# A segment-recurrent attention kernel: the last transpose and sum of each segment in two column halves, and the order of every engine written down whole

## The chip, the cores and the metric

The kernel runs on one core of one Trainium2 chip. The metric is device time in microseconds (us), from one launch to its end. Each kernel is run several times, and the median is compared.

## The reference

The input is 2048 tokens of 512 values. They go through a layer norm, then through an attention that runs over 64 segments of 32 tokens, one after the other, and at the end through a layer norm and an MLP. What matters here is the loop over the segments:

```python
mem = mem0                                            # 8 memory rows of 512
for s in range(64):
    h = concatenate([mem, x[32*s:32*s+32]])           # 40 rows
    q, k, v = h @ Wq, h @ Wk, h @ Wv                  # 32 heads of 128
    p = softmax(where(mask, q @ k.T * scale, -1e9))   # per head
    o = (p @ v) @ Wo                                  # 40 rows of 512
    mem = o[:8]                                       # feeds the next segment
    outs.append(o[8:])
```

The mask lets every row see the memory rows and, among the other 32, those up to itself. A segment can't begin before the memory rows of the one before are there; its other rows need nothing of it. Behind the loop stand `h = x + attention` and `h + MLP(layernorm(h))` with 1792 hidden values.

## The kernel before, in words

A segment has 8 memory rows (M) and 32 rows of x. 24 of the 32 (A) share a 32-row tile `hT` with the memory rows: `hT[:, slot, chunk, 0:24]` are x, `24:32` memory, with the 512 features in four chunks on the partitions. The last 8 x rows of four segments (B) are put together into one 32-row tile `hB`. So work goes by blocks of four segments, and the number of a segment modulo four is called its class here.

On TensorE (PE in the profile) a segment is a sequence of units. A unit of a projection is four matmuls of 512 columns, one per quarter of the array, over one of the four feature chunks. Each of Q0, Q1, K0, K1, V0, V1 (half of the heads each) is four such units on `hT`. F0 and F1 are units on `hB` or `OTB` that belong to the next block: its K in class 0, its Q in class 1, its V in class 2, and in class 3 the output projection of the B rows. They depend on nothing in the segment and fill gaps. SC0 and SC1 are the scores of the memory rows, PV0 and PV1 the products of their softmax with V, WO is the output projection (8 units of 16 matmuls of 256 columns), SA the scores of the A rows, and PVA their product with V, which belongs to the segment before: the A and B rows run one or more segments late, since only the memory rows are awaited.

The other engines carry results between these units. VectorE (DVE) and ScalarE (ACT) cast PSUM into SBUF (`kq`, `VS`, `OT`); VectorE transposes (`KALL`, `QT`, `PTC`, `PTA`, `QTB`). Names with m, x and B stand for the memory, A and B rows of one tile. The softmax of a half r (0 or 1) of the heads is, in order: `nmc` (negative maximum, VectorE), two Exps into `EC` (ScalarE; the code calls the parts Ea and EC), `rsc` and `PC` twice each (reciprocal, product), and `PTC` (transpose). The mask is copied into the scores' bank ahead of them (called SP0, SP1, for SA SAp). At the end of a segment VectorE transposes the result of WO out of PSUM into `TT` and adds the two halves of the heads with `halves_add`; the sums of the memory rows (called hTm) are written into the next segment's `hT`, those of the A rows (opA) into `opT`, later. GpSimd (POOL) does small copies (`ZC`, `BD`), the product `PA`, and the sums of `TTB`, the same result for the B rows, into `opT`. From there a DMA transpose (`oN`) takes a block back to rows of x.

All of this is recorded first, and a scheduler written in Python sets each engine's order before any instruction is emitted. TensorE's order is a table, `ORDERS`, one row a class, of (name, first unit, last unit). `PLAN` gives for many kinds of operation a due time in us after the segment's Q0, for each class; a segment counts `STEP` = 10.28. `HOME` pins a kind to an engine where two could do it, and the rest is decided by free time in the scheduler's own model. Some operations are kept back and recorded again behind another one (lists `late`, `now`, `turned`, `folds`). Each operation waits on a semaphore for what it reads; on its own engine too, for VectorE and GpSimd.

`align` counts TensorE's instructions and adds weight loads (the LDWEIGHTS without a matmul) until the first unit of a segment stands at a fixed place, modulo 256 instructions: `PHASE` = 0, 64, 128, 192 for classes 0 to 3. `KEEP` leaves out the weight load where the unit before has loaded the same chunk (`matmul_kept`, L606 in the profile).

Lines in the profile of before: L873 and L606 projections; L891 to L893 casts; L914 transposes of Q and K; L1042 scores; L1050 to L1069 softmax; L1080 and L1085 PV; L1110 to L1137 SA, its softmax, and `PTA`, `BD`; L1148 PVA; L1176 WO; L1188 the transpose into `TT`; L1182 every `halves_add`; L1219 to L1232 the B rows' sums; L1246 to L1260 the way back to rows.

Of the kernel before, what the change touches and what calls it, by code (L numbers as in the profile page):

```python
# [1694 lines left out]
```

## Time and profile before

| | |
|---|---|
| runs | 805.17, 806.22, 806.32 us; median 806.22 |
| profiled execution, first to last instruction | 804.0 us, 2.2 below the median |
| busy | PE 96%, DVE 77%, ACT 68%, POOL 44% of the span |
| until segment 1 begins | 51.96 us |
| segments 1 to 62 | 637.53 us (51.96 to 689.49), 10.28 each |
| last segment, MLP, output | 114.5 us |
| granted TensorE clock | 0.996 of full speed |

The profile shows one execution. In a row of the time line stand the start and the length in us, the engine, the line of the kernel, the operation, and what is written from what. Matmuls overlap in the records, so the distance between two starts tells more than a length. In a row of a group, the last numbers are the busy time in us with the mean of one in ns, and the idle time ahead of them.

### The profile page before, as it was taken

How to read it: one execution, taken by the hardware profiler on the slowest of the kernel's cores; microseconds unless marked ns; L12 is line 12 of the kernel's file. 1: busy time of each engine (PE TensorE's matmuls, PEld its weight loads, DVE VectorE, ACT ScalarE, POOL GpSimd, SP SyncE). 2: the span in 40 equal slices, each digit the busy share in tenths (PEclk: the TensorE clock that was granted, in tenths of full speed). 3: DMA queues.
4: the chain of work that ended last, by engine and by line, in shares of the span. 5: the costliest groups of instructions: out<-in, count | busy, mean ns of one | idle time of the engine just before them, and what ended most of it. 6: DMA issues, size and time to landing. Idle time of an engine off the chain costs nothing.

```text
span 804.0 us, 43669 instructions
## 1 busy us (share of the span) xinstructions
PE 772.7 (96%) x19317; PEld 419.3 (52%) x18821; DVE 616.6 (77%) x1975; ACT 543.0 (68%) x1618; POOL 350.7 (44%) x886
## 2 busy tenths in 40 slices
PE   3788999999999999999999999999999999999998
PEld 1345555555555555555555555555555555544443
DVE  3267898898989898998989898989898887824211
ACT  2456777777777777777777787777777777743342
POOL 5023334545454545454545454545463535367200
PEclk9999999999999999999999999999999999999999
DMA  9960010110101010101010102020212131264200
GB/s 338 393 188 16 4 30 11 27 34 23 37 18 42 18 43 14 46 10 47 8 50 10 49 11 51 10 51 3 51 29 63 37 87 32 89 167 132 69 27 26
DMA packets 65450, 48.04 MB, mean 60 GB/s; under 512 B 29028, under 2 KB 61676, under 8 KB 65260
## 3 DMA queue, kind: packets, MB, share of 16 engines
q1 hardware_dynamic: 64928, 44.98, 18.9%
q8 instruction: 150, 2.46, 1.3%
q14 instruction: 40, 0.33, 0.1%
q10 hardware_dynamic: 332, 0.27, 0.1%
HBM read 31.08 MB, written 8.13 MB: 49 GB/s over the span
## 4 chain that ended last, share of the span: by engine, by line
PE 91%; DVE 3%; DMA 2%; SPq 2%; ACT 1%; issue 0%
PE ps L873 43%; PE ps L1176 16%; PE ps L606 7%; PE quad L1584 6%; PE ps L1577 5%; PE ps L1215 4%; PE quad L1080 3%; DMA WQ<-in_A_Wq_dram 2%; SPq L776 2%; PE ps L1110 2%; PE quad L1042 2%; PE ps L1370 2%; PE quad L1148 1%; PE quad L1085 1%; DVE PC L1067 1%; ACT kq L891 1%
## 5 line engine op out<-in xcount | busy, mean ns | idle before, releaser
L873 PE MATMUL ps<-WQ,hT 128*32 128x512 bf16 x2048 | 157.0, 382 | 3.5 <-DVE hT L1182 3.3
L1176 PE MATMUL ps<-WO,OT 128*32 128x256 bf16 x4224 | 141.5, 275 | 1.0 <-ACT OT L891 1.0
L873 PE MATMUL ps<-WV,hT 128*32 128x512 bf16 x1780 | 138.1, 379 | 0.0
L892 ACT ACTIVATE kq<-ps 128x512 bf16<-128x512 f32 x146 | 87.2, 597 | 57.5 <-PE ps L873 57.2
L1131 POOL TENSOR_TENSOR PA<-SA,rsa 128x256 bf16<-128x256 f32 x64 | 39.8, 622 | 181.4 <-DVE rsa L1124 169.6
L891 ACT CAST kq<-ps 128x512 bf16<-128x512 f32 x160 | 93.3, 583 | 29.8 <-PE ps L873 29.8
L1176 PEld LDWEIGHTS ps<-WO,OT 128*32 128x32 bf16 x4224 | 96.2, 96 | 23.6 <-ACT OT L891 4.0
L1137 POOL COPY BD<-PTA 32x192 bf16<-32x192 bf16 x256 | 95.7, 374 | 16.5 <-DVE PTA L1133 0.8
L1067 DVE SCALAR_TENSOR_TENSOR PC<-EC,rsc,even 128x128 bf16<-128x128 f32 x256 | 94.5, 370 | 6.7
L873 PE MATMUL ps<-WK,hT 128*32 128x512 bf16 x1292 | 92.3, 379 | 0.0
L873 PEld LDWEIGHTS ps<-WQ,hT 128*32 128x32 bf16 x2048 | 56.4, 96 | 63.7 <-issue 19.3
L914 DVE STREAM_TRANSPOSE KALL<-kq 128x256 f32<-128x256 f32 x160 | 70.5, 441 | 21.3 <-ACT kq L891 19.0
L891 ACT CAST VS<-ps 128x512 bf16<-128x512 f32 x189 | 83.9, 444 | 0.9
L1059 ACT ACTIVATE EC<-quad,nmc 128x64 f32<-128x64 f32 x252 | 76.8, 310 | 5.7
L606 PE MATMUL ps<-WK,hT 128*32 128x512 bf16 x756 | 74.3, 379 | 0.0
L891 ACT CAST OT<-quad 128x128 bf16<-128x128 f32 (+1 forms) x208 | 68.4, 352 | 4.9 <-PE quad L1085 0.7
L914 DVE STREAM_TRANSPOSE QT<-kq 128x256 f32<-128x256 f32 x128 | 57.0, 446 | 16.1 <-ACT kq L892 15.0
L873 PEld LDWEIGHTS ps<-WV,hT 128*32 128x32 bf16 x1780 | 49.4, 96 | 34.9 <-issue 1.0
L1580 ACT ACTIVATE WQ<-ps,b1t 128x512 bf16<-128x512 f32 x42 | 28.9, 687 | 52.0 <-PE ps L1577 52.0
L1122 ACT ACTIVATE SA<-SA 128x256 f32<-128x256 f32 x64 | 26.7, 417 | 52.2 <-DVE SA L1121 48.8
L873 PEld LDWEIGHTS ps<-WK,hT 128*32 128x32 bf16 x1292 | 35.9, 97 | 46.6 <-issue 20.2
L1228 POOL TENSOR_TENSOR opT<-TTB,TTS 32x64 bf16<-32x64 f32 x128 | 40.3, 315 | 31.7 <-DVE opT L1182 22.5
(159 smaller groups left out, 1475.9 us busy)
## 6 DMA issues: line engine op xcount, KB each, us to landing
WV<-in_A_Wv_dram SPq DMA_DIRECT2D x4, 1024.0 KB, 10.4
WK<-in_A_Wk_dram SPq DMA_DIRECT2D x4, 1024.0 KB, 18.1
WQ<-in_A_Wq_dram SPq DMA_DIRECT2D x4, 1024.0 KB, 19.4
WO<-in_A_Wo_dram SPq DMA_DIRECT2D x16, 256.0 KB, 7.7
v_last<-VSB SPq DMA_DIRECT2D x60, 64.0 KB, 3.1
VBD<-v_last SPq DMA_DIRECT2D x60, 64.0 KB, 2.9
h_mid<-xr SPq DMA_DIRECT2D x16, 128.0 KB, 1.8
WQ<-h_mid SPq DMA_DIRECT2D x4, 512.0 KB, 4.4
```

What stands on the lines that cost most here:

```text
L606: return e.add_instruction(mybir.InstMatmult(name="I-%d" % (4000000 + _kept[0]), engine=mybir.EngineType.PE, start_tensor_calc=start, stop ...
L873: ins = e.matmul(o, l, m, start=(k == 0), stop=(k == DC - 1), tile_position=(0, 32 * j), skip_group_check=True)
L891: return {"act": (lambda e: e.copy(out, src), t_act(n, ps_)), "dve": (lambda e: e.tensor_copy(out, src), 0.155 + 1.0e-3 * n * fast)}
L892: return {"act": (lambda e: e.mul(out, src, scale_), t_act(n, ps_)), "dve": (lambda e: e.tensor_scalar(out, src, scale_, None, ALU.mult), ...
L914: S.op("dve", lambda e: e.transpose(out, src), reads=[("kq", i)], writes=[key], dur=t_dve(256) + 0.02)
L1059: return e.activation(EC[:, r, sl, :], o[:, sl, :], ACTF.Exp, bias=nmc[:, r, sl:sl + 1], accum_out=smc[:, r, sl:sl + 1])
L1067: S.op("dve", lambda e, sl=sl, xc=xc: e.scalar_tensor_tensor(PC[:, r, :, :, sl], xc, rsc[:, r, sl:sl + 1], ev, ALU.mult, ALU.mult), reads= ...
L1137: S.narrow(S.op("pool", lambda e, j=j, rows=rows: e.tensor_copy(BD[rows, par, :, j, :, :], PTA[rows, :, 0:NA, :]), reads=["PTA"], writes=[ ...
L1176: ins = e.matmul(ps[bank][32 * j:32 * j + 32, 0:256], lhs(slot(h)), wo_cols(h, b), start=(k == 0), stop=(k == 15), tile_position=(0, 32 * ...
L1228: return e.tensor_tensor(o[32 * q:32 * q + 32, c:c + 2], x, y, ALU.add)
L1577: ins = e.matmul(ps[bank][:, 0:SBT], W1[:, cc, fc * P:(fc + 1) * P], hnT_of(k)[:, cc, :], start=(cc == 0), stop=(cc == DC - 1))
L1584: S.op("pe", lambda e: e.matmul(quad[:, t, :], gT_of(k, fc)[:, t * P:(t + 1) * P], W2[:, fc, :], start=(fc == 0), stop=(fc == FC - 1)), re ...
```

## The change

1. The last step of a segment in halves. `wo` transposes columns 0 to 127 of the result, sums the memory rows of feature chunks 0 and 1 from them, and does the same for columns 128 to 255 and chunks 2 and 3. The keys of both are split, and the units of Q0, Q1 and K0 ask only for the half that their chunk lies in (`early`). `ORDERS` puts the units of chunks 0 and 1 of Q0 and K0 first.

```diff
-            S.op("dve", lambda e: e.transpose(tt..., ps[bank][:, 0:256]), reads=[("ps", bank)], writes=[("TT", par)], ...)
-            if mem:
-                sl = (s + 1) % RING
-                S.op("dve", lambda e: [halves_add(tt, q2, hT[64 * q2:64 * q2 + 64, sl, :, NA:SEG], slice(NA, SEG))(e) for q2 in range(2)][1],
-                     reads=[("TT", par)], writes=[("hTm", sl)], dur=0.4)
+            sl = (s + 1) % RING
+            for n in range(2):
+                c = slice(2 * n, 2 * n + 2)
+                S.op("dve", lambda e, n=n, c=c: e.transpose(tt[:, c]..., ps[bank][:, 128 * n:128 * n + 128]), reads=[("ps", bank)],
+                     writes=[("TT", par, n)], ...)
+                if mem:
+                    S.op("dve", lambda e, c=c: [halves_add(tt[:, c], q2, hT[64 * q2:64 * q2 + 64, sl, c, NA:SEG], slice(NA, SEG))(e) for q2 in range(2)][1],
+                         reads=[("TT", par, n)], writes=[("hTm", sl, n)], dur=0.36)
...
-                u = S.op("pe", f, reads=[(key, r, cc) for _, key, r, _, _ in parts] + reads, ...)
+                u = S.op("pe", f, reads=[(key, r, cc) for _, key, r, _, _ in parts] + reads + [("hTm", slot[1] % RING, n) for n in range(2) if slot[0] == "A" and (n == cc // 2 or not early)], ...)
```

2. The orders. `PLAN` now has a time for nearly every kind of operation and class, to three digits; `HOME` names an engine for every operation that could run on two; a new table `DUR` holds a duration for each. In segments 1 to 63 the operations of an engine are chained in the order of these times. The casts of the A rows into `OT` (OTx0, OTx1) are both on ScalarE in every class, and so are the mask of SA (SAp) and the casts of the next block's K and Q (kq4, kq5). Some rows of the tables, by class 0 to 3:

```diff
-        "SP1": (-1.16, -1.01, -1.18, -1.31),
-        "OTx1": (8.9, 8.39, 8.15, 8.0),
-        "TT": (9.37,) * 4,
-        "hTm": (9.86,) * 4,
+        'SP1': (-1.641, 0.904, -0.752, 4.445),
+        'OTx1': (10.663, 8.222, 7.108, 7.125),
+        'TT0': (9.285, 9.217, 9.233, 9.247),
+        'hTm0': (9.628, 9.683, 9.576, 9.713),
+        'TT1': (10.019, 9.45, 9.967, 9.48),
+        'hTm1': (10.362, 10.421, 10.31, 10.451),
...
-STEP = 10.28
-PHASE = (0, 64, 128, 192)
+STEP = 10.134
+PHASE = 88
```

In class 3 the mask SP1 (4.445) lies between the first half's Exps Ea0 (4.144) and EC0 (4.618). The lists of kept-back operations are gone, but for one of the A rows' sums. The sums of `TTB` on GpSimd are planned operations f0a to f13, due 12.1 to 41.7 us after the Q0 of their class-3 segment.

3. The scores and fillers on TensorE. In classes 1 to 3 five units stand between SC0 and SC1, six before. In class 0 one unit of F0 moves ahead of PV0 in exchange, and SA comes after two or three of the last fillers.

4. Blocks of instructions. `align` brings only the first segment of each block of four to a fixed place (88); the weight loads added for it are 327, 528 before.

```diff
-            if PHASE and o.tag is not None and o.tag[0] != seg:
-                seg = o.tag[0]
-                owed = (LATE.get(seg, PHASE[seg % 4]) - at) % FETCH_N
+            if o.tag is not None and o.tag[0] // 4 > seg:
+                seg = o.tag[0] // 4
+                owed = (PHASE - at) % FETCH_N
```

5. Waits. A read of a PSUM bank behind another read of it on the same engine no longer waits there (`soft`), GpSimd excepted.

The rows below show where these meet. First VectorE at the end of segment 37 (class 1), before; `QTB` belongs to the next block, `nma` and `SA` to the A rows' softmax.

```order
L1069 STREAM_TRANSPOSE PTC<-PC 128x128 [waits sem_dve]
L1182 TENSOR_TENSOR opT<-TT 64x4x24 [waits sem_dve]
L1182 TENSOR_TENSOR opT<-TT 64x4x24
L893 TENSOR_SCALAR kq<-ps 128x512 [waits sem_pe]
L914 STREAM_TRANSPOSE QTB<-kq 128x256 [waits sem_dve]
L1188 STREAM_TRANSPOSE TT<-ps 128x256 [waits sem_pe]
L1182 TENSOR_TENSOR hT<-TT 64x4x8 [waits sem_dve]
L1182 TENSOR_TENSOR hT<-TT 64x4x8
L1120 TENSOR_REDUCE nma<-ps 128x8 [waits sem_pe]
L1121 TENSOR_TENSOR SA<-ps,nma 128x256 [waits sem_dve]
```

The same place after:

```order
L1334 STREAM_TRANSPOSE PTC<-PC 128x128 [waits sem_dve]
L1147 STREAM_TRANSPOSE QTB<-kq 128x256 [waits sem_act]
L1446 TENSOR_TENSOR opT<-TT 64x4x24 x2
L1455 STREAM_TRANSPOSE TT<-ps 128x128 [waits sem_pe]
L1455 STREAM_TRANSPOSE TT<-ps 128x128
L1446 TENSOR_TENSOR hT<-TT 64x2x8 [waits sem_dve]
L1446 TENSOR_TENSOR hT<-TT 64x2x8
L1385 TENSOR_REDUCE nma<-ps 128x8 [waits sem_pe]
L1446 TENSOR_TENSOR hT<-TT 64x2x8 [waits sem_dve]
L1446 TENSOR_TENSOR hT<-TT 64x2x8
L1386 TENSOR_TENSOR SA<-ps,nma 128x256 [waits sem_dve]
```

One transpose and two sums have become two and four, and the cast `kq` has gone to ScalarE. In classes 1 and 3 both transposes stand ahead of the first sums, as here; in classes 0 and 2 the first sums stand between them.

VectorE in the softmax of the same segment, before:

```order
L914 STREAM_TRANSPOSE KALL<-kq 128x256 [waits sem_act]
L1064 RECIPROCAL rsc<-smc 128x1 [waits sem_act]
L1067 SCALAR_TENSOR_TENSOR PC<-EC,rsc,even 128x128 [waits sem_dve]
L1064 RECIPROCAL rsc<-smc 128x1 [waits sem_act]
L1050 TENSOR_REDUCE nmc<-quad 128x2 [waits sem_pe]
L1067 SCALAR_TENSOR_TENSOR PC<-EC,rsc,even 128x128 [waits sem_dve]
L1069 STREAM_TRANSPOSE PTC<-PC 128x128 [waits sem_dve]
```

After:

```order
L1147 STREAM_TRANSPOSE KALL<-kq 128x256 [waits sem_act]
L1324 RECIPROCAL rsc<-smc 128x1 [waits sem_act]
L1329 SCALAR_TENSOR_TENSOR PC<-EC,rsc,even 128x128 [waits sem_dve]
L1297 TENSOR_REDUCE nmc<-quad 128x2 [waits sem_pe]
L1324 RECIPROCAL rsc<-smc 128x1 [waits sem_act]
L1329 SCALAR_TENSOR_TENSOR PC<-EC,rsc,even 128x128 [waits sem_dve]
L1334 STREAM_TRANSPOSE PTC<-PC 128x128 [waits sem_dve]
```

The maximum of the second scores (`nmc`) has moved ahead of the first half's second reciprocal.

TensorE from the first scores to the first PV of segment 37, before:

```order
L1042 MATMUL quad<-KALL,ZC 32x64 x16
L873 MATMUL ps<-WV,hT 32x512 x4
L606 MATMUL ps<-WV,hT 32x512 x4
L873 MATMUL ps<-WV,hT 32x512 x12
L873 MATMUL ps<-WQ,hB 32x512 x4
L1042 MATMUL quad<-KALL,ZC 32x64 x16
L873 MATMUL ps<-WQ,hB 32x512 x4
L873 MATMUL ps<-WV,hT 32x512 x12
L873 MATMUL ps<-WQ,hB 32x512 x4
L1080 MATMUL quad<-PTC,VS 128x2x16 x8
```

After:

```order
L1289 MATMUL quad<-KALL,ZC 32x64 x16
L1106 MATMUL ps<-WV,hT 32x512 x16
L843 MATMUL ps<-WV,hT 32x512 x4
L1289 MATMUL quad<-KALL,ZC 32x64 x16
L1106 MATMUL ps<-WQ,hB 32x512 x4
L1106 MATMUL ps<-WV,hT 32x512 x12
L1106 MATMUL ps<-WQ,hB 32x512 x8
L1345 MATMUL quad<-PTC,VS 128x2x16 x8
```

One unit of the filler (`WQ,hB`) has gone from ahead of the second scores to behind them; the number of units ahead of PV0 is the same, eleven.

More of the change, by code (lines that the diff above doesn't have):

```diff
@@ L163, in op @@
                 deps.add(w)
+                if not (excl and w in self.lookers.get(k, ())):
+                    hard.add(w)
             if excl:
@@ L169, in op @@
                 deps.add(w)
+                hard.add(w)
             deps.update(self.readers.get(k, ()))
+            hard.update(self.readers.get(k, ()))
         deps.update(a for a in after if a is not None)
         deps.discard(o)
+        o.soft = deps - hard
+        for k in o.reads:
+            self.lookers.setdefault(k, set()).add(o)
+        for k in o.writes:
+            self.lookers[k] = set()
         o.deps = sorted(deps, key=lambda d: d.gidx)
@@ L245, in schedule @@
                 o.prev.succ.append(o)
+        rows = {e: [] for e in ENGINES}
+        for o in self.rec:
+            at = planned(o)
+            if at is not None and not o.is_dma:
+                o.eng = HOME.get((o.kind, o.tag[0] % 4), o.eng)
+                if o.alts:
+                    o.fn, o.dur = o.alts[o.eng]
+                o.dur = DUR.get((o.kind, o.eng), o.dur)
+                rows[o.eng].append((STEP * o.tag[0] + at, o.gidx, o))
+        for row in rows.values():
+            row.sort()
+            for a, b in zip(row, row[1:]):
+                b[2].order = a[2]
+                a[2].succ.append(b[2])
         topo, left = [], {}
@@ L252, in schedule @@
             topo.append(o)
-            for d in o.deps + ([o.prev] if o.prev is not None else []):
+            for d in o.deps + [p for p in (o.prev, o.order) if p is not None]:
                 left[d] -= 1
@@ L299, in schedule @@
             for d in o.deps:
-                t = max(t, d.start + d.dur + self.lat(d, o))
+                t = max(t, d.start + (0.0 if d.eng == o.eng and d in o.soft else d.dur + self.lat(d, o)))
+            if o.order is not None:
+                t = max(t, o.order.start + o.order.dur - OVERLAP[o.eng])
             if o.eng in ("sp", "act") and o.prev is not None:
@@ L578, with directions @@
 MC, MR, MF, MH = 1, 2, 3, 4
-def directions():
+def directions(order):
     back, last = {}, None
-    if not KEEP:
-        return {n: False for n, _, _ in ORDER}
-    for n, lo, hi in ORDER:
-        pack = "A" if n[0] in "KQV" else "B" if n[0] == "F" else None
-        if n[:2] in ("PV", "SC", "SA", "WO"):
-            pack = None
+    for n, lo, hi, was in order:
+        pack = ("A", was) if n in ("K0", "K1", "Q0", "Q1", "V0", "V1") else "B" if n[0] == "F" else None
+        for u in range(lo, hi if pack else lo):
+            if u == 0:
+                back[n] = last == (pack, DC - 1) and n not in ("Q0", "K0", "Q1")
+            last = pack, DC - 1 - u % DC if back.get(n, False) != (u >= DC) else u % DC
         if pack is None:
             last = None
-            continue
-        if n not in back:
-            back[n] = last is not None and last == (pack, DC - 1)
-        end = min(hi, DC) - 1
-        last = (pack, DC - 1 - end if back[n] else end)
     return back
@@ L799, in qbf @@
             return quad[:].bitcast(BF16)[:, :, 2 * c0:2 * c0 + P]
-        turned, held, late, now = [], [], [], []
+        held = []
         def ln1(tb, after=()):
@@ L1127, in sa_tail @@
             par = s % 2
-            after = [S.last_writer.get(("hTm", (s + 1) % RING))] if s + 1 < NS else []
             b = rsa[:]
@@ L1393, in build_kernel @@
         ln1(0)
-        back = directions()
+        backs = [directions(order) for order in ORDERS]
         for s in range(NS):
             bk, sg = s // 4, s % 4
+            back = backs[sg]
             if s > 0:
```

624 lines of the change are left out of this document (419 added, 205 removed), and 9 rows, old and new, of tables (EMIT, ORDERS).

## The prediction

> **What bounds the kernel now.** I read the page's head first, then the stretches by stage, then one segment on TensorE and VectorE instruction by instruction, then the prices of the instructions that the change touches.
>
> ```profile
> span 804.0 us, 43669 instructions
> PE 772.7 (96%) x19317; PEld 419.3 (52%) x18821; DVE 616.6 (77%) x1975; ACT 543.0 (68%) x1618; POOL 350.7 (44%) x886
> ```
>
> TensorE looks full. Three stretches say otherwise: segments 1 to 62 together, segment 2 alone, then segments 36 to 39 (classes 0, 1, 2, 3).
>
> ```profile
> 51.96:689.49 637.53, 631.63 (x17932) 354.00 (x17420) 563.52 (x1857) 477.43 (x1493) 302.48 (x776) 1.00 0.12 31
> ...
> 62.12:72.35 10.23, 8.91 (x261) 5.33 (x305) 7.71 (x27) 6.84 (x22) 4.55 (x12) 1.00 0.13 23
> ...
> 411.35:421.57 10.22, 10.22 (x296) 5.66 (x280) 9.07 (x31) 7.64 (x24) 4.97 (x13) 1.00 0.02 6
> 421.57:431.90 10.33, 10.33 (x296) 5.92 (x279) 9.43 (x31) 8.04 (x25) 5.24 (x14) 1.00 0.06 17
> 431.90:442.12 10.22, 10.22 (x296) 5.74 (x281) 9.32 (x32) 7.93 (x24) 5.70 (x15) 1.00 0.01 3
> 442.12:452.41 10.29, 10.29 (x296) 5.59 (x280) 9.10 (x31) 7.47 (x24) 4.43 (x12) 1.00 0.38 93
> ```
>
> Columns are length, then busy PE, PEld, DVE, ACT, POOL, the granted clock (1.00), DMA share. Segment 2 has none of the eight filler units F (projections for the next block). Its TensorE is busy 8.91 us, and it still lasts 10.23, as long as class 0 or 2 with all the filler. So a segment's length is set by its chain (project, score, softmax, output, back into the next projection), and the filler only covers it. 62 segments take 637.53 us, 10.28 each. That is the stretch the change works on. The 52.0 us ahead of it (segment 0, whose orders stay free) and the 114.5 behind (the MLP) I take as unchanged.
>
> Where the chain shows on TensorE, segment 37 (class 1):
>
> ```profile
> 424.38 0.83 PE L873 MATMUL ps<-WK,hT 128*32 128x512 bf16 x12
> 425.03 0.31 PE L1042 MATMUL quad<-KALL,ZC 128*32 128x64 bf16 x16
> ...
> 426.44 0.31 PE L1042 MATMUL quad<-KALL,ZC 128*32 128x64 bf16 x16
> ...
> 427.43 0.40 PE L873 MATMUL ps<-WQ,hB 128*32 128x512 bf16 x4
> 427.80 0.27 PE L1080 MATMUL quad<-PTC,VS 64*128 64x32 bf16 x8
> ...
> 428.50 0.61 PE L1176 MATMUL ps<-WO,OT 128*32 128x256 bf16 x16
> 429.06 0.27 PE L1080 MATMUL quad<-PTC,VS 64*128 64x32 bf16 x8
> ...
> 429.32 1.50 PE L1176 MATMUL ps<-WO,OT 128*32 128x256 bf16 x48
> 430.64 0.42 PE L1110 MATMUL ps<-KALL,QT 128*32 128x32 bf16 x32
> 430.89 1.06 PE L873 MATMUL ps<-WQ,hB 128*32 128x512 bf16 x16
> 431.90 0.40 PE L873 MATMUL ps<-WQ,hT 128*32 128x512 bf16 x4
> ```
>
> Read starts, not busy times (matmul records overlap). A unit of four 512-wide matmuls takes 0.216 (424.38 to 425.03 is three). Against that, three places are too long. The unit at 427.43 takes 0.37: 0.15 of waiting ahead of PV0. Sixteen WO matmuls should take a third of 1.32 (429.32 to 430.64), 0.44; from 428.50 to 429.06 is 0.56, so 0.12 ahead of PV1. Four units from 430.89 should end at 431.75; Q0 starts at 431.90: 0.15. Now who ends them:
>
> ```profile
> 424.42 0.45 DVE L914 STREAM_TRANSPOSE KALL<-kq 128x256 f32<-128x256 f32 x1
> 424.79 0.27 DVE L1133 STREAM_TRANSPOSE PTA<-PA 128x128 f32<-128x128 f32 x1
> ...
> 426.40 0.38 DVE L1067 SCALAR_TENSOR_TENSOR PC<-EC,rsc,even 128x128 bf16<-128x128 f32 x1
> 426.69 0.15 DVE L1064 RECIPROCAL rsc<-smc 128x1 f32<-128x1 f32 x1
> 426.83 0.29 DVE L1050 TENSOR_REDUCE nmc<-quad 128x2 f32<-128x128 f32 x1
> 427.04 0.36 DVE L1067 SCALAR_TENSOR_TENSOR PC<-EC,rsc,even 128x128 bf16<-128x128 f32 x1
> 427.43 0.31 DVE L1069 STREAM_TRANSPOSE PTC<-PC 128x128 f32<-128x128 f32 x1
> ...
> 428.69 0.31 DVE L1069 STREAM_TRANSPOSE PTC<-PC 128x128 f32<-128x128 f32 x1
> ...
> 430.87 0.45 DVE L1188 STREAM_TRANSPOSE TT<-ps 128x256 f32<-128x256 f32 x1
> 431.35 0.48 DVE L1182 TENSOR_TENSOR hT<-TT 64x32 bf16<-64x32 f32 x2
> ```
>
> PTC ends at 427.74 and 429.00, hT at 431.83; each time TensorE goes on 0.06 to 0.07 later. So VectorE ends all three waits, 0.42 us in this class, and no segment can gain much more than that.
>
> **The change, part by part.** Prices:
>
> ```profile
> L1069 DVE STREAM_TRANSPOSE PTC<-PC 128x128 f32<-128x128 f32 x128 | 39.9, 312 | 4.4
> L1182 DVE TENSOR_TENSOR opT<-TT 64x96 bf16<-64x96 f32 x128 | 34.3, 268 | 3.0
> L1188 DVE STREAM_TRANSPOSE TT<-ps 128x256 f32<-128x256 f32 x66 | 29.6, 449 | 22.4 <-PE ps L1176 19.2
> ...
> L891 DVE CAST OT<-quad 128x384 bf16<-128x384 f32 x48 | 25.7, 535 | 1.1 <-PE quad L1148 0.7
> ...
> L1182 DVE TENSOR_TENSOR hT<-TT 64x32 bf16<-64x32 f32 x126 | 25.1, 199 | 3.0
> ```
>
> 1. The halves. Before, from the last WO issue (430.64) to Q0: 0.23 until TT starts, 0.45, 0.03, 0.48, 0.07, in all 1.26. In the other classes it is 1.17, as in segment 36, where the unit that follows the last WO starts at 420.40 and the next segment at 421.57:
>
> ```profile
> 420.40 0.39 PE L873 MATMUL ps<-WK,hB 128*32 128x512 bf16 x4
> ```
>
> There the two sums take about the mean, 2 x 0.199 = 0.40, which is most of why class 1 lasts longest (10.33). A 128-wide TT: bounds 0.27 (PTA) and 0.449 (no saving); I take PTC's 0.312, the same shape and type. A half-width sum: 268 to 199 ns for 64 elements fewer, so 16 fewer than 32 give about 0.182, the pair 0.36; bounds 2 x 0.137 (half the elements of a mean 0.27) and today's slow 0.48. Where the first sum follows the first transpose (classes 0, 2): 0.23 + 0.31 + 0.03 + 0.36 + 0.07 = 1.00. Where the second transpose goes in between (1, 3): neighbours without a dependence overlap by 0.08 (424.42 + 0.45 against 424.79), so 0.23 + 0.23 + 0.23 + 0.36 + 0.07 = 1.12. The cover on TensorE is SA's 0.25 (430.64 to 430.89) plus four units, 1.11, and in class 0 three units, 0.90. So the distance becomes 1.00, 1.12, 1.11, 1.12: gains of 0.17, 0.14, 0.06, 0.05. The second half is wanted by the fifth unit, 0.86 after Q0; in class 1 it is done at about 1.83 against 1.98.
>
> [...]
>
> 2. Softmax order. In class 1 the second scores (426.44) now stand five units behind the first, not six, so their maximum can start 0.13 earlier, right behind the first PC, and the reciprocal goes after it. PTC0 ends about 0.06 later and PV0 with it. The second softmax, back to back at the end, gains 0.02 to 0.06 at PV1: 0.04. Class 2 gains 0.03 in the same way. In class 0 a unit more stands ahead of PV0 and takes the place of the wait there; PV1 stays with PTC1: 0. In class 3 the mask for the second scores is put between the two Exps, which eats what the fifth unit gives: 0.
>
> 3. Homes. Both OT casts of the A part go to ScalarE. VectorE loses 0.535 in 48 of 62 segments, 0.41 a segment, and gets 0.17 (transposes) + 0.33 (sums): 9.23 becomes about 9.3 of 10.1, still below the step. ScalarE goes from 7.8 to about 8.2; the casts stand around OTm1's, which I leave at its time: 0, or the 0.1 of being one cast late. In class 3 the late TT and the WO wait shrink a little, 0.04.
>
> 4. Pool's sums and oN. The last sums of a block move from the end of class 2 to about 1.4 us into class 3, so oN is issued there.
>
> ```profile
> L1246 SPq DMA_TRANSPOSE oN<-opT x16: 1196/1220/1298, 154.1 to 720.6; - x16
> ...
> DMA to landing us min/median/max: 2.4/2.5/4.2
> ```
>
> At worst it lands at 5.7, before PTC1 ends at 7.4, where its add stands: 0. The same holds for nma and SA, up to 0.2 later: PTA, which they feed, runs at 424.79 and is used after 427.80. Pads and the waits of VectorE on itself that go: 0, TensorE gains 0.01 at most.
>
> Sum: class 0 0.17, class 1 0.14 + 0.04, class 2 0.06 + 0.03, class 3 0.05 + 0.04: 0.53 in four segments, 15.5 times, 8.2 us. The profiled span of 804.0 becomes 795.8. The median of the runs, 806.22, lies 2.2 above that span, which stays: **798.0 us**. A measurement here can tell 0.2%, 1.6 us, from no change.
>
> **Rivals.** Slow halves: in 37 the pair took 0.48, not 0.40.
>
> ```profile
> L1182 DVE TENSOR_TENSOR hT<-TT x126: 186/189/349, 51.5 to 689.1; 64x32 bf16<-64x32 f32 x126
> ```
>
> Some single sums double. GpSimd now has its sums spread over the segments, so this may become the rule: 0.09 in classes 0, 1 and 3 is 4.2 us, giving 802.2. Against it: the median is 189, so few do today.
>
> Fixed price, on the slow side: if a half costs what the whole did, classes 1 and 3 get 0.23 + 0.37 + 0.37 + 0.40 + 0.07 = 1.44 for 1.26 and 1.17, class 0 and 2 nothing; with item 2 and the 0.04 kept this is 0.45 - 0.11 = 0.34 a block, 5 us, 811. It decides once a half transpose costs over about 0.40. PTC's 0.312 speaks against it. [...]
>
> Instruction blocks, on the slow side too:
>
> ```profile
> q8 instruction: 150, 2.46, 1.3%
> ```
>
> 38138 instructions of PE and PEld over 150 packets are 254 each. The kernel pads each segment so that its blocks begin at fixed places; the change does so once in four. There are 9 blocks in four segments, 140 in all; from 0.07 us each this turns the gain into a loss, and at PV0's 0.15 each it gives 819. Against it: today's nine places differ in each class and no unit outside the three waits is long.
>
> **Chances.** The sum as worked out (gain 4.7 to 12, 794.0 to 801.5): 0.70. Slow halves or one cast late, 801.5 to 804.6: 0.13. All eaten, within 0.2%: 0.06. Slower: blocks 0.07, fixed price 0.04. Faster is 0.83. The low end is the sum with 0.06 more at PV1 in each class (15.5 x 0.24 = 3.7 us); the high end takes in the slow halves: 794 to 804.5.
>
> **What would show it.** In the new profile: TT as 128x128 near 0.31, the sums near 0.18; from WO's last issue to Q0 1.0 in class 0 and 1.1 elsewhere; PV1 within 0.05 of 7.45 after Q0; segments of about 10.05, 10.15, 10.13 and 10.2. A new wait would show as a TensorE start that VectorE's PTC or hT doesn't explain: an OT cast ahead of WO, the mask ahead of the second scores in class 3, or gaps at no releaser every 256 instructions. I am wrong if a segment still lasts 10.28 although the halves are fast.

## The result, and the profile after

The changed kernel takes 818.89 us (median; 818.56 to 819.84), beside 805.69 for the kernel before on the same chip: a ratio of 1.0166, 95% interval 1.0154 to 1.0179. It is slower by 13 us, where 8 less was forecast. The head of the page, the chain that ended last, and the stretches: segments 1 to 62, segments 36 to 39 (classes 0 to 3), and segments 55 to 62 (columns as in the prediction).

```profile
span 817.0 us, 43561 instructions
PE 779.2 (95%) x19317; PEld 405.1 (50%) x18508; DVE 603.8 (74%) x2086; ACT 563.2 (69%) x1699; POOL 341.9 (42%) x886
...
PE 64%; DVE 22%; ACT 8%; DMA 3%; SPq 2%; issue 1%; POOL 0%
```

```profile
50.52:702.20 651.68, 638.53 (x17932) 340.68 (x17164) 549.14 (x1958) 497.61 (x1573) 291.29 (x769) 1.00 0.13 30
417.19:427.40 10.21, 10.21 (x296) 5.54 (x282) 8.94 (x33) 7.27 (x23) 4.95 (x12) 1.00 0.06 18
427.40:438.02 10.62, 10.44 (x296) 5.30 (x277) 9.16 (x33) 8.92 (x28) 3.84 (x11) 1.00 0.06 16
438.02:448.40 10.38, 10.38 (x296) 5.78 (x289) 8.44 (x32) 8.40 (x27) 6.22 (x16) 1.00 0.01 3
448.40:459.04 10.64, 10.49 (x304) 5.45 (x278) 9.31 (x34) 7.77 (x25) 4.74 (x13) 1.00 0.39 71
615.86:702.20 86.34, 81.73 (x2264) 43.13 (x2150) 70.36 (x250) 63.34 (x202) 36.91 (x98) 1.00 0.20 53
```

The last row's stretch took this long before:

```profile
606.78:689.49 82.71, 80.99 (x2256) 44.70 (x2259) 70.03 (x237) 61.01 (x191) 37.93 (x98) 1.00 0.20 54
```

The loss is in the loop: 637.53 has become 651.68. Of these 14.1 us, 3.6 are in segments 55 to 62 and 10.5 in the 54 ahead, in classes 1, 2 and 3. Segment 0 has become 1.4 shorter (its granted TensorE clock is at 0.5 for 3.4 us, before for 6.8), and what stands behind the loop 0.3 longer. VectorE is less busy than before and yet holds 22% of the chain, 3% before: it isn't loaded, it is late. The table gives times after each segment's Q0, medians over segments 4 to 58, worked from the records of both traces:

| class | PV0 starts, before / after | last WO matmul starts to next Q0 | segment |
|---|---|---|---|
| 0 | 6.21 / 6.41 | 1.27 / 1.09 | 10.22 / 10.23 |
| 1 | 6.23 / 6.59 | 1.36 / 1.28 | 10.33 / 10.62 |
| 2 | 6.21 / 6.35 | 1.26 / 1.26 | 10.22 / 10.38 |
| 3 | 6.22 / 6.59 | 1.27 / 1.32 | 10.29 / 10.64 |

So PV0 is late in every class, by 0.14 to 0.37, and the halves win it back at the end in class 0 alone. Segment 37 (class 1), TensorE, VectorE, ScalarE, GpSimd; a bracket gives the idle time ahead of a row and what ended it:

```profile
432.21 0.31 PE L1289 MATMUL quad<-KALL,ZC 128*32 128x64 bf16 x16
...
433.21 0.61 PE L1106 MATMUL ps<-WQ,hB 128*32 128x512 bf16 x8
433.99 0.27 PE L1345 MATMUL quad<-PTC,VS 64*128 64x32 bf16 x8 [0.18 <-DVE rsc L1324]
```

```profile
431.75 0.41 DVE L1147 STREAM_TRANSPOSE KALL<-kq 128x256 f32<-128x256 f32 x1
432.08 0.16 DVE L1324 RECIPROCAL rsc<-smc 128x1 f32<-128x1 f32 x1
432.27 0.51 DVE L1329 SCALAR_TENSOR_TENSOR PC<-EC,rsc,even 128x128 bf16<-128x128 f32 x1
432.69 0.28 DVE L1297 TENSOR_REDUCE nmc<-quad 128x2 f32<-128x128 f32 x1
432.89 0.15 DVE L1324 RECIPROCAL rsc<-smc 128x1 f32<-128x1 f32 x1
433.07 0.52 DVE L1329 SCALAR_TENSOR_TENSOR PC<-EC,rsc,even 128x128 bf16<-128x128 f32 x1
433.62 0.31 DVE L1334 STREAM_TRANSPOSE PTC<-PC 128x128 f32<-128x128 f32 x1
```

```profile
429.04 0.42 ACT L1387 ACTIVATE SA<-SA 128x256 f32<-128x256 f32 x1 [0.18 <-DVE SA L1386]
429.36 0.58 ACT L1125 ACTIVATE kq<-ps 128x512 bf16<-128x512 f32 x1
...
432.14 0.20 ACT L1306 ACTIVATION_READ_ACCUMULATOR EC<-quad,nmc 128x1 f32 x1
```

```profile
431.88 1.55 POOL L1401 COPY BD<-PTA 32x192 bf16<-32x192 bf16 x4
```

Four things are in these rows. The second scores start 0.05 after their transpose `KALL` ends (432.16): they wait for it, and a filler unit less ahead of them buys nothing. The second reciprocal (432.89) stands behind the maximum, though its input was there at 432.34. Both PC take 0.51 and 0.52, not 0.38 and 0.36 as in segment 37 before; a copy on GpSimd starts at 431.88 and every 0.40 after, so at 432.28 and 433.08, each time with a PC. And kq2 (the cast `kq` at 429.36), which starts at 1.96 after Q0 and not at 1.74, stands behind the Exp of the A rows, which the second half's sums have made late.

Segment 38 (class 2) shows what no VectorE row explains:

```profile
443.61 0.62 PE L1106 MATMUL ps<-WV,hB 128*32 128x512 bf16 x8
444.04 0.41 PE L1106 MATMUL ps<-WV,hT 128*32 128x512 bf16 x4
444.38 0.27 PE L1345 MATMUL quad<-PTC,VS 64*128 64x32 bf16 x8
...
445.11 0.61 PE L1440 MATMUL ps<-WO,OT 128*32 128x256 bf16 x16
445.65 0.27 PE L1345 MATMUL quad<-PTC,VS 64*128 64x32 bf16 x8
```

```profile
443.87 0.31 DVE L1334 STREAM_TRANSPOSE PTC<-PC 128x128 f32<-128x128 f32 x1
...
445.12 0.31 DVE L1334 STREAM_TRANSPOSE PTC<-PC 128x128 f32<-128x128 f32 x1
```

PTC0 is done at 444.18, and still the unit at 444.04 takes 0.34 until PV0, 0.12 over its 0.216. PTC1 is done at 445.43, 0.22 ahead of PV1, and the sixteen WO matmuls take 0.54, not 0.44. No producer's row ends in these 0.10 to 0.12 ahead of the 64-row tiles of PV; they are called TensorE's own from here on. Over segments 4 to 57 they are 0.10 to 0.11 in the median of each class in which PTC is over 0.18 to 0.26 earlier. The prediction had put them down to VectorE.

The halves, first in segment 36 (class 0), then 37 (class 1), and their groups:

```profile
426.64 0.32 DVE L1455 STREAM_TRANSPOSE TT<-ps 128x128 f32<-128x128 f32 x1 [0.45 <-PE ps L1440]
427.00 0.35 DVE L1446 TENSOR_TENSOR hT<-TT 64x16 bf16<-64x16 f32 x2
...
437.06 0.51 DVE L1455 STREAM_TRANSPOSE TT<-ps 128x128 f32<-128x128 f32 x2 [0.55 <-PE ps L1440]
437.61 0.36 DVE L1446 TENSOR_TENSOR hT<-TT 64x16 bf16<-64x16 f32 x2
438.00 0.42 DVE L1385 TENSOR_REDUCE nma<-ps 128x8 f32<-128x256 f32 x1
```

```profile
L1446 DVE TENSOR_TENSOR hT<-TT 64x16 bf16<-64x16 f32 x252 | 43.7, 174 | 5.8
L1455 DVE STREAM_TRANSPOSE TT<-ps 128x128 f32<-128x128 f32 x132 | 37.7, 305 | 59.4 <-PE ps L1440 58.3
```

They cost what was forecast, 0.305 and 0.174. In class 1 the sums start when both transposes are over (437.57), not after the first.

In segments 55 to 62 the largest single loss is segment 55, which takes 11.81 us and took 10.29. TensorE and VectorE at its end:

```profile
627.67 0.41 PE L1106 MATMUL ps<-WQ,hT 128*32 128x512 bf16 x4 [1.08 <-DVE hT L1446]
```

```profile
624.83 0.52 DVE L1446 TENSOR_TENSOR opT<-TT 64x96 bf16<-64x96 f32 x2 [1.38 <-DMA oN<-opT]
625.36 0.42 DVE L1505 TENSOR_TENSOR xr<-xr,oN 128x512 bf16<-128x512 bf16 x1
...
626.69 0.50 DVE L1455 STREAM_TRANSPOSE TT<-ps 128x128 f32<-128x128 f32 x2
```

The transfer `oN` was issued 5.11 us after Q0 there, not at 1.8 as in the blocks before (segments 15 to 51), and landed at 8.94. VectorE waits for it in its written order, with TT behind.

### The profile page after: what moved, and what is told of

Read it like the earlier page. It is cut to its first block, busy times and chain, and to the rows that moved or that the text cites. A ratio compares the mean times of both kernels' runs of the same rounds, so it can differ in the third digit from the quotient of the medians.

```text
span 817.0 us, 43561 instructions
## 1 busy us (share of the span) xinstructions
PE 779.2 (95%) x19317; PEld 405.1 (50%) x18508; DVE 603.8 (74%) x2086; ACT 563.2 (69%) x1699; POOL 341.9 (42%) x886
## 4 chain that ended last, share of the span: by engine, by line
PE 64%; DVE 22%; ACT 8%; DMA 3%; SPq 2%; issue 1%; POOL 0%
PE ps L1106 23%; PE ps L1440 15%; PE quad L1828 6%; DVE PC L1329 5%; PE ps L1821 5%; ACT kq L1125 4%; PE ps L843 3%; PE quad L1345 3%; DVE hT L1446 3%; DVE TT L1455 2%; DMA WQ<-in_A_Wq_dram 2%; PE ps L1479 2%; SPq L1014 2%; ACT kq L1124 2%; DVE QT L1147 2%; DVE nmc L1297 2%
## 5 line engine op out<-in xcount | busy, mean ns | idle before, releaser
L1106 PE MATMUL ps<-WQ,hT 128*32 128x512 bf16 x1864 | 143.6, 380 | 4.0 <-DVE hT L1446 4.0
L1175 POOL COPY ZC<-QT 128x128 bf16<-128x128 bf16 x126 | 36.8, 292 | 214.4 <-DVE QT L1147 208.8
L1124 ACT CAST OT<-quad 128x128 bf16<-128x128 f32 (+1 forms) x255 | 95.3, 380 | 24.6 <-PE quad L1350 18.6
L1125 ACT ACTIVATE kq<-ps 128x512 bf16<-128x512 f32 x160 | 94.9, 593 | 23.8 <-PE ps L1106 23.6
L1329 DVE SCALAR_TENSOR_TENSOR PC<-EC,rsc,even 128x128 bf16<-128x128 f32 x256 | 104.9, 422 | 5.5
L1106 PE MATMUL ps<-WK,hT 128*32 128x512 bf16 x1356 | 101.1, 379 | 0.0
L1401 POOL COPY BD<-PTA 32x192 bf16<-32x192 bf16 x256 | 88.6, 346 | 23.3 <-DVE PTA L1397 7.6
L1106 PEld LDWEIGHTS ps<-WQ,hT 128*32 128x32 bf16 x1864 | 47.3, 96 | 73.0 <-DVE hT L1446 21.2
L1455 DVE STREAM_TRANSPOSE TT<-ps 128x128 f32<-128x128 f32 x132 | 37.7, 305 | 59.4 <-PE ps L1440 58.3
L843 PE MATMUL ps<-WK,hT 128*32 128x512 bf16 x692 | 68.3, 379 | 0.0
L1147 DVE STREAM_TRANSPOSE QT<-kq 128x256 f32<-128x256 f32 x128 | 55.3, 432 | 6.3 <-ACT kq L1125 2.0
## 6 DMA issues: line engine op xcount, KB each, us to landing
WV<-in_A_Wv_dram SPq DMA_DIRECT2D x4, 1024.0 KB, 10.5
```

The lines of the kernel that those rows point to most:

```text
L843: return e.add_instruction(mybir.InstMatmult(name="I-%d" % (4000000 + _kept[0]), engine=mybir.EngineType.PE, start_tensor_calc=start, stop ...
L1106: ins = e.matmul(o, l, m, start=(k == 0), stop=(k == DC - 1), tile_position=(0, 32 * j), skip_group_check=True)
L1124: return {"act": (lambda e: e.copy(out, src), t_act(n, ps_)), "dve": (lambda e: e.tensor_copy(out, src), 0.155 + 1.0e-3 * n * fast)}
L1125: return {"act": (lambda e: e.mul(out, src, scale_), t_act(n, ps_)), "dve": (lambda e: e.tensor_scalar(out, src, scale_, None, ALU.mult), ...
L1147: S.op("dve", lambda e: e.transpose(out, src), reads=[("kq", i)], writes=[key] + list(more), dur=t_dve(256) + 0.02)
L1329: return e.scalar_tensor_tensor(PC[:, r, :, :, sl], xc, rsc[:, r, sl:sl + 1], ev, ALU.mult, ALU.mult)
```

## The experiments

The order theory: the time goes where an instruction of a written order stands ahead of one that is ready, on the path to PV0. Its first rival: instruction blocks, whose forecast of 819 is the time that came out. Steps (the lengths of segments) below are medians by class, 0 to 3, from each trace.

**Blocks (e1).** Each segment back to its place.

```diff
-            if o.tag is not None and o.tag[0] // 4 > seg:
+            if o.tag is not None and o.tag[0] != seg:
...
-                owed = (PHASE - at) % FETCH_N
+                owed = ({60: 60}.get(seg, (0, 64, 128, 192)[seg % 4]) - at) % FETCH_N
```

> The changed kernel, but with each segment again brought to a fixed place (0, 64, 128, 192 modulo 256 instructions), nothing else. Block theory (instruction blocks that begin in the middle of a segment cost TensorE about 0.1 us each): the time falls by 8 to 13 us, to 806 to 811. Order theory (the loss comes from what stands where on VectorE, ScalarE and TensorE, not from blocks): 819 within 1.5 us, PV0 stays at 6.41, 6.59, 6.35 and 6.59 us after Q0 in classes 0 to 3.

Measured: 818.38, ratio 1.0155 (1.0132 to 1.0178), PV0 at 6.42, 6.55, 6.34, 6.59. Segments 1 to 54 take 565.6, in the changed kernel 565.3. The block theory falls; its 819 was a coincidence. Segment 55 lasts 10.72 here: `oN` went out at 0.92 and landed at 4.12. So some 1.1 of the 3.6 us in the last segments is this late transfer.

**The reciprocal first (e2).**

```diff
-        'rsc0': (5.133, 5.331, 5.103, 5.361),
+        'rsc0': (5.133, 5.101, 5.103, 5.131),
```

> The changed kernel, with the second reciprocal of the first scores (rsc0) back ahead of the second scores' maximum (nmc1) on VectorE in classes 1 and 3. Order theory: PC0 starts 0.18 us sooner and no longer together with a copy on GpSimd, so it takes 0.37 and not 0.52 to 0.57; PTC0 ends near 6.2, and PV0 comes at 6.35, where TensorE itself is ready. That is 0.24 in each of two classes, 0.48 x 15.5 = 7 us: 812, between 809 and 814. Block theory, or a theory that the halves at the segment's end cost the time: no change, 819.

Measured: 815.33, 1.0114 (1.0088 to 1.0140). This is outside the 809 to 814 that was expected. PV0 comes at 6.34 and 6.38 in classes 1 and 3, and the second PC of a segment (PC1 from here on) takes 0.35. The steps fall by 0.18 and 0.13, not by 0.24: from PV0 to WO it now takes 0.78, since the next things are late.

**Fillers as before (e3).**

```diff
-('V1', 0, 1, 0), ('SC1', 0, 1, 0), ('F1', 0, 1, 0),          # class 1; 3 alike, in 2 a unit of V1 moves
+('V1', 0, 1, 0), ('F1', 0, 1, 0), ('SC1', 0, 1, 0),
...
-('F0', 0, 1, 0), ('V1', 2, 4, 0), ('F1', 1, 3, 0), ('PV0', 0, 1, 0),   # class 0
+('V1', 2, 4, 0), ('F1', 1, 3, 0), ('PV0', 0, 1, 0),                    # F0 behind WO
```

> The changed kernel, with the fillers on TensorE split as before: six units between the two scores and five from there to PV0, in all classes. Order theory: in classes 0 and 2 PV0 goes back from 6.41 and 6.35 to 6.21, because the second scores wait for the transpose of K1 (it ends at 4.75) and gain 0.06 only by standing a unit sooner, while the unit put behind them costs its whole 0.216. In class 2 the step falls by 0.14; in class 0 the unit comes back behind WO, where it costs what it saved, so 10.2 stays. Classes 1 and 3 hang on VectorE's order and stay. In all 0.14 to 0.2 a block, 2 to 3 us: 816. The reading of the prediction (the 0.15 ahead of PV0 is a wait for VectorE, and a unit there is free): PV0 hardly moves, 819.

Measured: 818.48, 1.0165 (1.0141 to 1.0190). PV0 goes to 6.21 and 6.23 in classes 0 and 2, as the order theory says, and the time doesn't: in class 2 WO still starts at 7.09, since PVA waits, and in class 0 the unit is back behind WO, where the distance to Q0 grows from 1.09 to 1.21.

**Three orders undone (e4).** The two above, and in class 3 the mask SP1 from 4.445 to -0.45, out of the pair of Exps.

> The changed kernel with three orders put back together: six units between the scores, the reciprocal ahead of the maximum, and in class 3 the mask of the second scores (SP1) out of the pair of Exps, put at the end of the segment before. The halves, the casts' homes, the planned sums and the blocks stay as changed. Order theory: PV0 near 6.21 in all four classes, steps near 10.20, 10.26, 10.24 and 10.27, 41.86 - 40.97 = 0.89 a block, 14 us: 805, as fast as before. If the halves or the blocks cost something by themselves it stays above 810.

Measured: 812.20, 1.0088 (1.0063 to 1.0114). PV0 at 6.21, 6.23, 6.22, 6.25: all of its lateness is these three orders. Yet half the loss stays; segment 39 there shows the next wait:

```profile
449.83 0.27 PE L1345 MATMUL quad<-PTC,VS 64*128 64x32 bf16 x8
...
450.21 0.38 PE L1412 MATMUL quad<-BD,VS 64*128 64x48 bf16 x16
...
449.20 0.46 POOL L1182 COPY ZC<-QTB 128x256 bf16<-128x256 bf16 x1
449.72 0.34 POOL L1401 COPY BD<-PTA 32x192 bf16<-32x192 bf16 x1
```

The last BD copy ends at 450.06, behind a copy for the next block, and PVA starts 0.15 later; before, it followed PV0 by 0.17 (here 0.38).

**One unit more ahead of PV0, in the kernel before (e5).**

```diff
-('PV0', 0, 99), ('PVA', 0, 99), ('F1', 3, 4), ('WO', 0, 2)          # classes 1 and 2; 0 and 3 alike
+('F1', 3, 4), ('PV0', 0, 99), ('PVA', 0, 99), ('WO', 0, 2)
```

> The kernel before, with the filler unit that stands behind PVA put ahead of PV0 in all four classes, so that twelve units stand between the first scores and PV0 and not eleven. The question is what the 0.15 us ahead of PV0 is. If it is a wait for VectorE (as the prediction read it), the unit takes the wait's place and PV0 comes 0.07 later, at 6.28. If 0.11 of it is TensorE's own, a price of going from the 32-column tiles of the units to the 64-row tiles of PV, PV0 comes 0.19 to 0.2 later, at 6.40 to 6.41, while VectorE's PTC0 ends at 6.15 as before. The segments last as long as before either way, since WO then starts sooner by the unit that has gone.

Measured: 817.38 (one run; before 805.33). In all four classes PV0 starts at 6.41. A segment of class 0:

```profile
422.80 0.61 PE L873 MATMUL ps<-WK,hB 128*32 128x512 bf16 x8
423.35 0.27 PE L1080 MATMUL quad<-PTC,VS 64*128 64x32 bf16 x8
...
424.09 0.62 PE L1176 MATMUL ps<-WO,OT 128*32 128x256 bf16 x16 [0.22 <-ACT OT L891]
```

```profile
422.77 0.31 DVE L1069 STREAM_TRANSPOSE PTC<-PC 128x128 f32<-128x128 f32 x1
```

PTC0 ends at 423.08, and two units that should take 0.43 together still take 0.55. The cast `VS` that PV0 reads ended 0.9 before it. So the 0.12 is TensorE's own, and the disputed term is 0.20 a unit, not 0. The expectation that segments keep their length was wrong: they last 10.46 to 10.49. The unit behind PVA had covered the cast OTm0, for which WO now waits.

**The halves alone, in the kernel before (e6).** `wo` and `passes` as in the change's first part; due times TT0 9.37, hTm0 9.7, TT1 9.95, hTm1 10.1.

> The kernel before with the first part of the change alone: the last transpose and the sums in two halves, in the order transpose, sums, transpose, sums, and Q0, Q1 and K0 reading the half that they need. Orders, homes, blocks and fillers stay. Reading of the prediction: the chain from WO to Q0 shrinks by 0.17 and by up to 0.25 in class 1, of which TensorE's cover (SA and four units, 1.11 from the last WO's end) leaves 0.06, 0.15, 0.05 and 0.06: 0.32 a block, 5 us, 800.5. Order theory: the same bound, less what comes late behind it: nma and the A rows' softmax start 0.2 later, which reaches kq2 or BD in one class or two: 0.1 to 0.3 a block gained, 802 to 804. If the halves cost something by themselves (a fixed price of the smaller instructions), 806 or more.

Measured: 831.40, 1.0321 (1.0303 to 1.0338), far above the 800.5 to 804 of the first two readings; the third, a fixed price of the halves, had 806 or more. But from WO to Q0 it takes less than before (1.19 to 1.32), so such a price isn't the cause. TensorE and VectorE at the start of segment 36:

```profile
426.24 0.49 PE L875 MATMUL ps<-WQ,hT 128*32 128x512 bf16 x4
426.90 0.62 PE L875 MATMUL ps<-WQ,hT 128*32 128x512 bf16 x8 [0.17 <-DVE SA L1123]
...
425.96 0.42 DVE L1122 TENSOR_REDUCE nma<-ps 128x8 f32<-128x256 f32 x1
426.42 0.42 DVE L1123 TENSOR_TENSOR SA<-ps,nma 128x256 f32<-128x256 f32 x1
```

The unit at 426.24 should end at 426.46; Q1, which writes the PSUM bank of SA, waits until 426.90 for SA's readers, which have moved behind the second half's sums.

**The same with K0 ahead of Q1 (e11)**, as the change orders them.

```diff
-('Q0', 2, 3), ('Q1', 0, 1), ('Q0', 3, 4), ('K0', 2, 4), ('Q1', 1, 4)
+('Q0', 2, 3), ('K0', 2, 3), ('Q0', 3, 4), ('K0', 3, 4), ('Q1', 0, 4)
```

> The kernel before with the halves, and with K0's units ahead of Q1's on TensorE, as the changed kernel has them. With the halves alone the first unit of Q1 waited 0.46 us, since it writes the PSUM bank (5) that SA uses, and the A rows' maximum and difference (nma, SAs), which read it, had moved behind the second half's sums. With Q1 last the bank is free in time. What stays: the Exp of the A rows (SAe) ends at 1.9 and kq2, due at 1.75, comes 0.1 to 0.2 later, against 0.03 to 0.07 gained from WO to Q0: 0.1 to 0.5 a block lost, 807 to 813. If the bank isn't the cause, 831 stays. If the halves pay as the prediction reckoned them once nothing stands in their way, 800 to 804.

Measured: 825.24, 1.0247 (1.0228 to 1.0267). The bank was part of it; the first scores are still 0.17 to 0.31 late, behind the A rows' Exp on ScalarE, and PC1 now meets a BD copy (0.48 to 0.52). Of the forecast 0.17, 0.14, 0.06 and 0.05, the distance from WO to Q0 shows 0.05, 0.01, 0.02 and 0.07. The halves alone don't pay in the old orders.

**The halves undone, in the changed kernel (e10).** One transpose of 256 columns, two sums of 32.

> The changed kernel with the last transpose and sums whole again (one transpose of 256 columns, two sums of 32 columns), everything else as changed. Order theory: the halves do what they should where VectorE is what Q0 waits for, 0.19 in class 0 and 0.08 in class 1; classes 2 and 3 have little of it. Taken away, 0.27 a block is lost and a little comes back since the A rows' softmax starts sooner: 0 to 4 us slower than the changed kernel, 819 to 823. If the halves are what makes the changed kernel slow, it is faster, below 817.

Measured: 821.71, 1.0193 (1.0168 to 1.0218), 2.8 more than the changed kernel, though the intervals overlap. From WO to Q0 class 0 goes back from 1.09 to 1.25. In class 1 the step falls, from 10.62 to 10.53, since the first scores come back from 3.55 to 3.46: there the halves do cost, by what they push behind them. Taken together they are no cause of the loss.

**A needless copy on GpSimd, in the kernel before (e9).**

```diff
...                                   # and the other three copies of BD wait for it
+                if j == 0:
+                    S.op("pool", lambda e: e.tensor_copy(junk[:], ident[:]), reads=[("BD", par, 0), "ident"], writes=["junk"], dur=0.29)
```

> The kernel before with one needless copy of 128x128 on GpSimd behind the first of the four BD copies, so that the other three start about 0.35 us later; nothing else is asked of anyone. In the traces so far PC takes 0.37 us, but 0.47 to 0.57 wherever an instruction on GpSimd starts within 0.04 of PC's own start, and no more than 0.38 where one starts 0.06 or more to either side. If that coincidence is the cause, the BD copy that now starts near 5.45 meets PC1 (5.45) and lengthens it to about 0.5, PTC0 ends 0.13 later and each segment lasts about as much longer: 8 us, 813. If GpSimd's running beside it mattered and not the start, PC0 and PC1 would not change (GpSimd is as busy there today), 806. A PVA that waits for the last BD shows as a gap ahead of PVA and would have to be told apart in the trace.

Measured: 814.09 (one run; before 805.70). VectorE and GpSimd in a segment of class 0:

```profile
420.83 0.36 DVE L1068 SCALAR_TENSOR_TENSOR PC<-EC,rsc,even 128x128 bf16<-128x128 f32 x1
...
421.44 0.53 DVE L1068 SCALAR_TENSOR_TENSOR PC<-EC,rsc,even 128x128 bf16<-128x128 f32 x1
...
420.71 0.29 POOL L1140 COPY junk<-ident 128x128 bf16<-128x128 bf16 x1
421.06 1.15 POOL L1138 COPY BD<-PTA 32x192 bf16<-32x192 bf16 x3
```

The three copies stand 0.40 apart; the second starts at 421.46, with the PC that takes 0.53. The PC at 420.83 runs beside the needless copy, which began 0.12 earlier, and takes 0.36. PVA follows PV0 by 0.17, as before, so it isn't waiting for the last copy. Steps rise by 0.14 to 0.17. Shown: a copy on GpSimd that starts with PC lengthens it, from 0.36 to 0.53; what decides is in the last section.

**Six orders changed (e7).** To the three: class 1's VS1 from 6.301 to 6.701, behind OTm0; on GpSimd f01 from 34.225 to 36.62 and class 0's ZCb from -4.581 to -3.9, both behind BD.

> The changed kernel with the three orders of the run before last put back, and three more that its trace shows as the next waits: in class 1 the cast of V1 (VS1) behind OTm0 on ScalarE; on GpSimd the sum f01 out of the way of BD in class 2, and the copy ZCb of the next block behind the last BD in class 3. Order theory: PVA starts 0.06 behind PV0's last matmul in all classes again, and WO 0.69 behind PV0: class 1 falls by 0.12, class 2 by 0.15, class 3 by 0.2: 0.47 a block, 7 us, 805 from 812. If the wait ahead of PVA isn't for BD, no change in classes 2 and 3, 810.

Measured: 811.55, 1.0066 (1.0041 to 1.0091), not 805. From PV0 to WO it takes 0.69 to 0.70 in all classes, as expected, and segments 1 to 54 fall from 558.7 to 556.0. Segments 55 to 62 rise from 86.1 to 89.6. In the medians of the runs this is 0.65 less than e4, and the ranges overlap.

**The first sums between the transposes also in classes 1 and 3 (e8)** (hTm0 9.44 and 9.47).

> As the kernel beside it with six orders changed, and also in classes 1 and 3 the first sums between the two transposes, as in classes 0 and 2. Order theory: the distance from the last WO matmul's start to Q0 falls from 1.28 and 1.32 to the 1.25 at which TensorE is itself ready: 0.1 a block, 1.5 us, 803.5. If the sums wait for the second transpose in any case, no change against its neighbour.

Measured: 808.54, 1.0047 (1.0030 to 1.0063). From WO to Q0 it is 1.20 and 1.22: the sums do wait for whichever transpose stands ahead. But the steps of classes 2 and 0 rise by 0.08 and 0.15, since their first scores come at 3.54 and 3.55 and not at 3.46: from the last WO matmul to the next segment's first scores it takes as long as in e7, to 0.01, and the A rows' softmax now sets it. Segments 1 to 54 take 555.5 (e7 556.0, before 554.8); most of the 3.0 us to e7 stand in segments 55 to 62 (86.8 for 89.6). This is the fastest of the repaired kernels. In segments 1 to 54 the changed kernel lost 10.5: three orders gave back 6.7, the next three 2.6, the sums 0.6.

**Two more, on top of e8 (e12)** (SP0 to 0.45 in classes 0 and 2, f01 to 32.6).

> The fastest of the repaired kernels so far (808.5), with two more orders: on ScalarE the mask SP0 ahead of the A rows' Exp in classes 0 and 2, so that kq2 follows that Exp at once, and on GpSimd the sum f01 into the idle time at 2.2 in class 2 and no longer behind BD. Order theory: the first scores come back from 3.55 and 3.54 to 3.47 in classes 0 and 2, 0.16 a block, 2.5 us; the last block's early transposes, which wait for the sums, give back some of the 3 us that segment 60 lost: 803 to 806, level with before or just under it. If SC0 waits for something else, 808.

Measured: 812.23, 1.0090 (1.0059 to 1.0120), a miss. SC0 still comes at 3.55 and 3.54 in classes 0 and 2, though in class 2 kq2 now starts at 1.70: the next thing in line holds it. In class 0 GpSimd's copy ZC ends at 3.40 after Q0 and not at 3.18, behind the A rows' PA (2.56 to 3.17); in class 2 VectorE takes the A rows' sum (`sma`) until 2.66, with QT and KALL behind it. Three segments of class 0 last 10.98.

**The tail left to the scheduler (e13).**

```diff
-... or o.tag[0] < (8 if o.kind in LOOSE else 1):
+... or o.tag[0] < (8 if o.kind in LOOSE else 1) or o.tag[0] > 53:
```

> The fastest repaired kernel (808.5), with the orders of segments 54 to 63 left to the scheduler's own choice and not written down; TensorE's order stays. In the traces segments 1 to 54 take 554.8 us before and 555.5 in the repaired kernel, and segments 55 to 62 take 82.7 and 86.8: what is still lost is there. Theory that the written orders are wrong where the loop's end differs from its middle (in segment 55 TT stands on VectorE behind an addition that waits for a transfer): those eight segments fall to 83 to 84.5 us, 805 to 806.5. Theory that the halves or TensorE's order cost it there: no change, 808 to 809.

Measured: 835.73, 1.0357 (1.0328 to 1.0386). Segments 55 to 62 take 109.3, not 84, but the run says little of its theories: the granted TensorE clock falls to 0.5 in nine stretches of 3.4 us between 618 and 731 us. In e8 there is one such stretch, in segment 60 (669.1 to 672.5), behind a PV0 that starts 0.86 after PTC0 and waits for a transfer into `VBD`. That segment takes 2.4 of the 4.0 us that e8 loses at the end, and segment 55 takes 1.7, with `oN` landing at 9.25. In the loop of the changed kernel the clock is 1.00 throughout. Why the transfers come late there was not tested.

**The kernel before with two waits taken away (e14)**: one of GpSimd's sums from class 1 to class 2, SP0 behind OTm1 in class 3.

> The kernel before with two small moves that its trace points to. In class 1 the first of the two last sums takes 0.275 us and not 0.187, beside a copy on GpSimd that starts 0.16 earlier; that copy goes to class 2. In class 3 the mask SP0 stands ahead of OTm1 on ScalarE, and WO waits 0.06; it goes behind. If these are the causes, class 1 falls by 0.09 (or by 0.06, where TensorE is ready) and class 3 by 0.06: 0.12 to 0.15 a block, 2 us, 803.5, a ratio of 0.9975 that five rounds can just tell. If the copy only moves its trouble to class 2, no change.

Measured: 805.00, 0.9994 (0.9985 to 1.0003). Class 1 falls from 10.33 to 10.24 as expected; class 2 gives back 0.04 (there a sum takes 0.24 now), and class 3 gets 0.06 longer. WO ends 0.06 sooner there, but VectorE is busy until TT, and an A rows' sum of 0.38, not 0.26, makes TT later still. No version beat the kernel before.

## Why the prediction was wrong, step by step

- **"So VectorE ends all three waits, 0.42 us in this class."** This step failed. It was read from the distance of two rows, and the rest of a unit's price wasn't looked for. In a block PV0 is late by 1.07 us in all; 0.34 of it hangs on this step, and 0.73 on item 2's orders in classes 1 and 3, the next steps that failed. Of 0.15 ahead of PV0 some 0.12 is TensorE's own, of 0.12 ahead of PV1 some 0.10; VectorE's part is 0.03 and 0.02, and only Q0's wait is real. Two terms hang on it. Class 0's twelfth unit, put at 0, costs 0.20, which is all that the halves win there. In class 2 the unit behind the second scores costs 0.14 at PV0, put at a gain of 0.03; the step gets it back only when BD is out of the way too (e3, e7). e5 and segment 38 show those 0.10 to 0.12 with PTC done 0.20 to 0.27 earlier; what TensorE does in them no run shows.
- **Item 2, "their maximum can start 0.13 earlier" and "PTC0 ends about 0.06 later".** This term failed too, and it weighs most. The scores came 0.06 sooner, since they wait for `KALL`. PTC0 ended 0.36 later: 0.03 of the maximum's start, 0.18 of the reciprocal behind it (PC starts at 5.67, not 5.47), 0.16 of PC's length. e2 gave 0.25 of it back at PV0.
- **The rival of slow halves** had the right suspect and the wrong victim. The sums in halves are not slow; PC is, 422 ns in the mean and not 370. The cause that the prediction suspected, GpSimd, is the same.
- **Item 2, class 3, "0".** The mask put the second Exp from 4.48 to 4.67; with the reciprocal that is 0.37 at PV0.
- **"The same holds for nma and SA", 0.** Wrong: the queue of ScalarE was not followed. The Exp of the A rows now ends after kq2 is due, 0.10 at SC0 in class 1; and BD, fed by the same chain, became the next wait (e4, e7).
- **Item 1.** Sizes right (0.312 forecast, 0.305; 0.182, 0.174), and class 0's 0.17 was 0.18, though the first scores of the segment behind it come 0.10 later, which leaves 0.09 from the last WO matmul to them. In class 1 it gave 0.08, not 0.14: the sums begin 0.30 after the second transpose, not 0.23. Class 2 got nothing, and class 3 lost 0.05.
- **Item 3, "0, or the 0.1 of being one cast late", and item 4, "0".** In class 1 a cast of V, written ahead of OTm0 on ScalarE, costs 0.12 from PV0 to WO as soon as PV0 is early (0.81 in e4, 0.70 in e7). The transfer `oN` was to land at 5.7 at worst; in segment 55 it lands at 8.94, and TT stands behind its add.
- **Blocks and fixed price**, the two rivals on the slow side: both out, by e1 and e10.
- **Chances.** No rival had a written order as its mechanism. Edits were put at 0 because each had slack; what a queue passes on was looked up for the first neighbour only.

The sum as it came, in a block: 0.00, +0.29, +0.16, +0.35 is 0.80, for 54 segments 10.8 of the measured 10.5.

## What to carry to other kernels

A unit that starts right after its producer doesn't prove that the gap ahead of it is the producer's: here PV0 followed PTC0 by 0.06 and owed 0.12 of 0.15 to itself. Look for a place in the trace where the producer is early, and subtract what the gap is there. A written order turns every estimate of a start into a wait: for each moved instruction, list what is ready behind it on its engine. And where a chain was tuned to within 0.03 us of TensorE, as here, a moved filler finds no free place: a unit more cost 0.20 at PV0 in class 0 and 0.14 in class 2. A shift of 0.03 us between VectorE and GpSimd changed which of the two waited: in segment 37 the last BD copy began 0.045 after PC before, and 0.013 after it in the changed kernel.
